# Normalising every tile in full before the turn, and finishing q at once, in a linear-attention and SwiGLU block

## Chip, cores, metric

One core of one Trainium2 chip (trn2). The metric is the device time of one execution in microseconds. The *span* of an execution is the stretch from its first to its last recorded instruction; the time is a little longer than the span.

## The reference, cut to what matters

```python
xn = layernorm(x)                                  # x: 2048 x 512, bf16
q, k, v = split(xn @ wqkv)                         # 32 heads of 16
phi = lambda t: where(t > 0, t + 1, exp(t)) + 1e-6
kv = einsum("bhsd,bhse->bhde", phi(k), v)
z  = sum over s of phi(k)
o  = (phi(q) kv) / (phi(q) z + 1e-6)
return x + o @ wo + (silu(xn @ w_gate) * (xn @ w_up)) @ w_down
```

The kernel works on 16 tiles of 128 rows. For the front of the program, each tile is normalised, turned (its columns must lie on the partitions), projected to k and q, and k and q go through phi. `G = xn^T phi(k)` is summed over the tiles in four PSUM banks. Then follow 56 gate and up groups, the division and the output tiles.

## The kernel before

The program is a list of operations; each engine runs its own in the order of the list and waits for what it depends on. The front is one text of letters with tile numbers. The letters that matter: S statistics, R 1/std, L/P/A normalise on VectorE/POOL/ACT, D turn by a DMA transpose, K/k and Q/q project to k and q, x/m/s phi of k (exp on ACT, min on POOL, sum on VectorE), y/n/u the same for q, z park q, G the G matmuls of a tile, F fillers.

```python
CENTRED = (0, 1)
NWARM = 8
...
def centre_half(t, h):                 # x - mean only: needs no 1/std
    K.add("dve", lambda e: e.tensor_scalar(
        out=xc[:, t, h * H:(h + 1) * H], in0=x_sb[:, t, h * H:(h + 1) * H], scalar1=mv[:, t, 0:1], scalar2=None,
        op0=ALU.subtract), r=xk(t) + [("mv", t)], w=[("xc", t, h)])
...
def nextbank():                        # projections share banks 4 to 7 in turn
    ring[0] += 1
    return 4 + (ring[0] - 1) % 4
...
def phi_keep(t):                       # park q in fp32, so that the bank comes free
    b, slot = at[0, t], later[t]
    K.add("act", lambda e: e.activation(tq[slot], banks[b][:, :], ACT.Copy), r=[B(b)], w=[("tq", slot)])

def phi_exp(i, t):
    ...
    if t in CENTRED:                   # the missing 1/std enters here
        K.add("act", lambda e: e.activation(buf, banks[b][:, :], ACT.Exp, bias=lstd[:, t:t + 1], scale=rstd[:, t:t + 1]),
              r=[B(b), ("rs", t), ("lstd", t)], w=[bkey])
    else:
        K.add("act", lambda e: e.activation(buf, banks[b][:, :], ACT.Exp), r=[B(b)], w=[bkey])
...
run("""
    S0 R0 b0 a0 d0 S1 M1 c0 F4 r0 C1 R1 g0 J0 W1 f0 K0 S2 r1 v1 k0 o1 S3 J1 R2 K1 x0 k1 L2 Q1 o0 x1 S4
    X2 m0 Q0 Y2 q1 m1 s0 R3 q0 R4 k2 L3 y1 s1 D3 P4 G0 S8 x2 z1 m2 D4 q2 S12 R8 z0 s2 G1 P8 y0 S14 G2
    ...
    s7 m6 q6 y7 L0 u8 D0 n7 q11 y6 s6 n6 G13 u7 y11 u6 n11 G5 u11 G14 u9 G11 u2 u1 G8 u0 G15 G7 G9 G10
    G4 G6
""")
```

Tiles 0 and 1 are only centred, and turned and projected so; the scale 1/std comes in afterwards, in phi and in a second, scaled copy for G. They are normalised again later, since the gate stage needs them. q of tiles 0, 1, 2, 8 and 9 is parked, and its sum runs late.

## Time and profile before

| | before |
|---|---|
| time, median of the first 3 executions | 213.36 us (213.19 to 213.69) |
| profiled execution | time 212.38 us, span 211.1 us |
| TensorE busy in the span | 98% |
| first projection | 6.09 us |
| first gate matmul | 48.09 us |

TensorE streams from the first projection on, one matmul of 512 columns each 0.216 us. So a hole in that stream, or a later start, is time lost, and work on the other engines is worth what it does to the stream. The lines that carry this are in the prediction.

### The profile page before, as it was taken

How to read it: one execution, taken by the hardware profiler on the slowest of the kernel's cores; microseconds unless marked ns; L12 is line 12 of the kernel's file. 1: busy time of each engine (PE TensorE's matmuls, PEld its weight loads, DVE VectorE, ACT ScalarE, POOL GpSimd, SP SyncE). 2: the span in 40 equal slices, each digit the busy share in tenths (PEclk: the TensorE clock that was granted, in tenths of full speed). 3: DMA queues.
4: the chain of work that ended last, by engine and by line, in shares of the span. 5: the costliest groups of instructions: out<-in, count | busy, mean ns of one | idle time of the engine just before them, and what ended most of it. 6: DMA issues, size and time to landing. Idle time of an engine off the chain costs nothing.

```text
span 211.1 us, 2717 instructions
## 1 busy us (share of the span) xinstructions
PE 207.3 (98%) x989; PEld 96.5 (46%) x1008; DVE 133.7 (63%) x225; ACT 69.8 (33%) x145; POOL 66.1 (31%) x91
## 2 busy tenths in 40 slices
PE   8999999999999999999999999999999999999996
PEld 3444444444544444444444444444444444444455
DVE  3998998965765379746546585755648754625122
ACT  4999986306363333031221322130123031220000
POOL 3789887999200252202202121202202220000000
PEclk9999999999999999999999999999999999999999
DMA  6954541499911301112011021011010111011101
GB/s 185 357 129 101 72 82 26 116 380 374 354 46 25 53 0 27 31 41 53 0 50 26 23 30 50 0 50 25 28 50 0 26 50 50 6 47 28 47 25 53
DMA packets 28829, 16.43 MB, mean 78 GB/s; under 512 B 18576, under 2 KB 28688, under 8 KB 28816
## 3 DMA queue, kind: packets, MB, share of 16 engines
q1 hardware_dynamic: 27984, 15.54, 27.3%
q10 hardware_dynamic: 832, 0.72, 1.0%
q8 instruction: 8, 0.13, 0.3%
q14 instruction: 5, 0.04, 0.1%
HBM read 9.96 MB, written 2.10 MB: 57 GB/s over the span
## 4 chain that ended last, share of the span: by engine, by line
PE 94%; DVE 2%; POOL 1%; issue 1%; ACT 1%; DVEq 0%
PE pb L521 45%; PE pb L619 23%; PE pb L390 10%; PE pb L615 6%; PE pb L439 6%; PE pb L247 2%; PE pb L357 1%; DVE stats L257 1%; POOL ef L418 1%; DVE pk L429 1%; ACT ef L411 1%; PE pb L546 1%; PE pb L609 0%; POOL xn L345 0%; DVE pq L429 0%
## 5 line engine op out<-in xcount | busy, mean ns | idle before, releaser
L529 ACT ACTIVATE sil<-pb 128x512 bf16<-128x512 f32 x56 | 33.3, 597 | 102.4 <-PE pb L521 98.7
L534 DVE TENSOR_TENSOR hT<-pb,sil 128x512 bf16<-128x512 f32 x56 | 38.2, 689 | 42.6 <-PE pb L521 39.9
L521 PE MATMUL pb<-xnT,wu 128*128 128x512 bf16 x223 | 57.5, 379 | 0.1
L521 PE MATMUL pb<-xnT,wg 128*128 128x512 bf16 x216 | 57.2, 379 | 0.4
L579 POOL TENSOR_TENSOR pz<-pq,zbc 128x512 f32<-128x512 bf16 x16 | 22.2, 1390 | 97.8 <-DVE den L586 79.6
L619 PE MATMUL pb<-wd,hT 128*128 128x512 bf16 (+2 forms) x249 | 51.0, 355 | 0.2
L619 PEld LDWEIGHTS pb<-wd,hT 128*128 128x128 bf16 x252 | 23.6, 98 | 24.9
L521 PEld LDWEIGHTS pb<-xnT,wu 128*128 128x128 bf16 x224 | 21.8, 98 | 26.4 <-DVE hT L534 1.4
L521 PEld LDWEIGHTS pb<-xnT,wg 128*128 128x128 bf16 x224 | 21.9, 98 | 25.8
L625 DVE TENSOR_TENSOR out_sb<-pb,x_sb 128x512 bf16<-128x512 f32 (+2 forms) x18 | 11.4, 632 | 23.1 <-PE pb L619 23.1
L390 PE MATMUL pb<-wqkv,xnT 128*128 128x512 bf16 x109 | 24.8, 379 | 0.2
L598 DVE TENSOR_TENSOR pq<-pq,rden 128x512 bf16<-128x512 bf16 x16 | 20.7, 1292 | 0.6
L418 POOL TENSOR_SCALAR ef<-ef 128x512 bf16<-128x512 bf16 x25 | 15.6, 628 | 4.3 <-ACT ef L411 3.9
L390 PEld LDWEIGHTS pb<-wqkv,xnT 128*128 128x128 bf16 x112 | 10.9, 98 | 13.3 <-DVE pk L429 0.5
L615 PE MATMUL pb<-M,pk 128*128 128x512 bf16 (+2 forms) x69 | 16.4, 354 | 0.2
L411 ACT ACTIVATE ef<-pb 128x512 bf16<-128x512 f32 x25 | 14.7, 591 | 3.5 <-PE pb L390 3.4
L257 DVE BATCH_NORM_STATS2 stats<-x_sb 128x6 f32<-128x512 bf16 x16 | 10.8, 677 | 3.3 <-DMA x_sb<-in_A_x_dram 3.1
L439 PE MATMUL pb<-pk,xn 128*128 128x512 bf16 x55 | 12.7, 379 | 0.1
L586 DVE TENSOR_REDUCE den<-pz 128x32 f32<-128x512 f32 x16 | 10.8, 675 | 0.0
L462 POOL TENSOR_TENSOR zacc<-zacc,pk 128x512 f32<-128x512 f32 x8 | 10.2, 1277 | 0.6
L615 PEld LDWEIGHTS pb<-M,pk 128*128 128x128 bf16 x72 | 6.8, 98 | 7.4
L429 DVE SCALAR_TENSOR_TENSOR pk<-pb,ef 128x512 bf16<-128x512 f32 x14 | 9.5, 681 | 1.0 <-POOL ef L418 0.8
(74 smaller groups left out, 111.3 us busy)
## 6 DMA issues: line engine op xcount, KB each, us to landing
out_dram<-out_sb SPq DMA_DIRECT2D x15, 128.0 KB, 1.9
x_sb<-in_A_x_dram SPq DMA_DIRECT2D x14, 128.0 KB, 4.3
wg<-in_B_w_gate_dram SPq DMA_DIRECT2D x2, 896.0 KB, 8.4
wu<-in_B_w_up_dram SPq DMA_DIRECT2D x2, 896.0 KB, 9.8
wd<-in_B_w_down_dram SPq DMA_DIRECT2D x2, 896.0 KB, 14.0
wqkv<-in_A_wqkv_dram ACTq DMA_DIRECT2D x2, 256.0 KB, 4.4
wqkv<-in_A_wqkv_dram SPq DMA_DIRECT2D x2, 256.0 KB, 4.7
wqkv<-in_A_wqkv_dram SPq DMA_DIRECT2D x1, 512.0 KB, 7.8
```

The source lines that it names most:

```text
L257: K.add("dve", lambda e: e.bn_stats(stats[:, t, :], x_sb[:, t, :]), r=xk(t), w=[("st", t)])
L390: K.add("pe", [(lambda e, c=c: e.matmul(banks[b][:, :], src[:, c, t * P:(t + 1) * P], wqkv[:, c, col:col + D], start=(c == 0), stop=(c == ...
L411: K.add("act", lambda e: e.activation(buf, banks[b][:, :], ACT.Exp), r=[B(b)], w=[bkey])
L418: K.add("pool", lambda e: e.tensor_scalar(out=buf, in0=buf, scalar1=top, scalar2=0.0, op0=ALU.min, op1=ALU.max), r=[bkey] + tkeys, w=[bkey])
L439: K.add("pe", [(lambda e, c=c: e.matmul(banks[c][:, :], src[:, t, c * P:(c + 1) * P], pk[:, t, :], start=first, stop=last)) for c in range ...
L521: fns.append(lambda e, c=c, b=b, w_=w_: e.matmul(banks[b][:, :], w_[:, c, fc * P:(fc + 1) * P], xnT[:, c, C * 512:(C + 1) * 512], start=(c ...
L529: K.add("act", lambda e: e.activation(sil[:, j % 2, :], banks[gb(j)][:, :], ACT.Silu), r=[B(gb(j))], w=[("sil", j % 2)])
L534: K.add("dve", lambda e: e.tensor_tensor(out=hT[:, C % 2, fc, :], in0=banks[gb(j) + 1][:, :], in1=sil[:, j % 2, :], op=ALU.mult), r=[B(gb( ...
L579: K.add("pool", lambda e: e.tensor_tensor(out=pz[:, t % 2, :].rearrange("q (g p) -> q g p", g=NG), in0=pq[:, t, :].rearrange("q (g p) -> q ...
L598: K.add("dve", lambda e: e.tensor_tensor(out=heads(pq[:, t, :]), in0=heads(pq[:, t, :]), in1=rden[:, i, :][:, :, None].broadcast_to([P, NH ...
L615: fns = [(lambda e, g=g: e.matmul(banks[bank][:, 0:hi - lo], pk[:, t, g * P:(g + 1) * P], M[:, g, lo:hi], start=(g == 0), stop=False)) for ...
L619: fns = [(lambda e, fc=fc: e.matmul(banks[bank][:, 0:hi - lo], hT[:, C % 2, fc, jj * P:(jj + 1) * P], wd[:, fc, lo:hi], start=False, stop= ...
```

## The change

The intent is a simpler front: every tile is normalised in full and then turned, and q of every tile is turned into phi at once. No centred tile, no parked copy, none of the small powers of std. The warm-up has ten matmuls instead of eight, the fillers are two instead of four, and the order of the whole front is a new one. Two DMA transposes fewer are issued, since tiles 0 and 1 are turned only once. The diff, cut to its core:

```diff
-CENTRED = (0, 1)
-NWARM = 8
+NWARM = 10
...
         def transp(t, b, lo=0, hi=NDC):
             tb = tview(b, hi - lo)
-            src = xc if t in CENTRED else xn
...
-        def phi_keep(t):
-            b, slot = at[0, t], later[t]
-            K.add("act", lambda e: e.activation(tq[slot], banks[b][:, :], ACT.Copy), r=[B(b)], w=[("tq", slot)])
...
         def phi_exp(i, t):
             b = at[i, t]
-            if t in CENTRED:
-                K.add("act", lambda e: e.activation(buf, banks[b][:, :], ACT.Exp, bias=lstd[:, t:t + 1], scale=rstd[:, t:t + 1]),
-                      r=[B(b), ("rs", t), ("lstd", t)], w=[bkey])
-            else:
-                K.add("act", lambda e: e.activation(buf, banks[b][:, :], ACT.Exp), r=[B(b)], w=[bkey])
+            K.add("act", lambda e: e.activation(ef[:, b - 4, :], banks[b][:, :], ACT.Exp), r=[B(b)], w=[("ef", b - 4)])
...
         run("""
-            S0 R0 b0 a0 d0 S1 M1 c0 F4 r0 C1 R1 g0 J0 W1 f0 K0 S2 r1 v1 k0 o1 S3 J1 R2 K1 x0 k1 L2 Q1 o0 x1 S4
...
+            S0 R0 S1 L0 R1 L1 S2 T0 E0 F2 T1 V1 R2 L2 k0 k1 x0 m0 S3 T2 S4 x1 m1 E2 R4 s0 q1 R3 L4 k2 x2 N3 A3
+            q2 s1 m2 y1 S5 R5 G0 D4 S6 s2 n1 G1 q0 y2 G2 D3 u1 R6 q4 N5 A5 S8 y0 k3 n2 N6 A6 u2 k4 y4 x3 n0 x4
+            n4 m3 u0 m4 S13 D5 q3 R8 u4 s3 P8 D6 S7 k5 y3 R13 D8 n3 G3 s4 x5 k6 R7 S9 R9 N7 q6 G4 m5 A7 u3 s5
...
+            x12 m12 k13 k15 n11 x15 m15 u11 G10 x13 m13 s12 G11 q15 q14 y15 n15 s13 s15 k14 x14 m14 y14 q12 s14
+            G12 y12 n12 n14 u15 G13 G14 u14 u12 G15
         """)
```

(T turns a tile on TensorE, E and V copy the turned tile out on ACT and VectorE.) With the parked sums gone, the G groups stand between the projections from the first tile on.

## The prediction

> **What bounds the kernel now.** I read first the page's shares, then the chain of work that ended last, then the order of time of the opening, then a table of stretches.
>
> ```profile
> PE 207.3 (98%) x989; PEld 96.5 (46%) x1008; DVE 133.7 (63%) x225; ACT 69.8 (33%) x145; POOL 66.1 (31%) x91
> PE   8999999999999999999999999999999999999996
> ```
>
> TensorE is busy 98% of the span, in every slice. Since a busy PE need not be at its peak, the chain decides:
>
> ```profile
> PE 94%; DVE 2%; POOL 1%; issue 1%; ACT 1%; DVEq 0%
> ...
> 6.30 2.45 PE pb L390 x10
> 8.75 0.22 PE pb L357 x4
> 8.97 2.16 PE pb L390 x10
> ...
> 44.64 3.62 PE pb L439 x16
> 48.25 3.67 PE pb L521 x17
> ```
>
> Ten projection matmuls take 2.16 us: one each 0.216 us, with no hole. The other engines appear in the chain only between 15.5 and 23 us, while TensorE is busy anyway. So after the opening the time is a count of matmuls. From the first projection (6.09 us) to the first gate matmul (48.09 us) lie 128 projection and 64 G matmuls (16 tiles x 12): 192 x 0.2158 = 41.43 us, plus one turned tile in the middle (0.22 us) and 0.35 us because the first few ran slow: 42.0 us, just what lies between. Everything before 6.09 us is warm-up and the way to the first turned tile:
>
> ```profile
> 3.12 0.69 DVE L257 BATCH_NORM_STATS2 stats<-x_sb 128x6 f32<-128x512 bf16 x1 [3.12 <-DMA x_sb<-in_A_x_dram]
> 3.85 0.18 DVE L260 BATCH_NORM_AGGREGATE mv<-stats 128x2 f32<-128x6 f32 x1
> 4.07 0.48 DVE L289 TENSOR_SCALAR hT<-x_sb,mv 128x256 bf16<-128x256 bf16 x2
> 4.07 0.29 ACT L264 ACTIVATE lnv<-mv,eps 128x1 f32<-128x1 f32 x1 [1.99 <-DVE mv L260]
> 4.39 0.20 ACT L266 ACTIVATE rstd<-lnv 128x1 f32<-128x1 f32 x1
> 4.41 0.61 PE L357 MATMUL pb<-ident,hT 128*128 128x128 bf16 x4
> 5.52 0.48 DVE L367 COPY hT<-pb 128x256 bf16<-128x256 bf16 x2
> 6.09 2.65 PE L390 MATMUL pb<-wqkv,hT 128*128 128x512 bf16 x10
> ```
>
> Tile 0 is only centred (4.07), so it need not wait for 1/std (ready at 4.59); it is turned and copied in halves, and the first projection starts at 6.09.
>
> **What the Trainium skill says.** (1) "TensorE: Matmul & The Clock Gate", Part 1, says that the array starts at half clock and is released after a sustained busy window of about 3.4 us, which runs freely, so that the moment varies. The trace agrees: the warm-up matmuls stand 0.427 us apart, the projections at 6.09 and 6.52 too, and from about 6.8 us on the distance is 0.216. (2) Part 4 of the same page says that transposes do not count as busy in the same way. No run here shows it yet; it matters because the new opening keeps two fillers where four stood. (3) "ScalarE: Activation LUTs", What ACT_TABLE_LOAD costs: a pointer operand adds about 93 ns to an ACTIVATE. The trace agrees: the exp of a centred tile, with pointer scale and bias, took 771 ns against 591 without. (4) "PSUM — Partial Sum Buffer", the section on bank collisions, asks for guarding by bank. The kernel does so, so the ring of four projection banks can make TensorE wait for the sum of phi on VectorE.
>
> **The change, part by part.**
>
> Off the path. Removed: five copies of q to fp32 on ACT (5 x 594 ns = 3.0 us); five late sums on VectorE (3.3 + 2.4 us), which become ordinary ones (5 x 686 ns), a relief of 2.3 us; the scaled start of the z sum on POOL (0.7 + 1.2 + 1.57 us, replaced by one 1.28 us add); the small powers, floors and caps; the separate xg (2 x 762 ns on POOL) and the second normalising of tiles 0 and 1; two of 15 DMA transposes. All this lies beside TensorE, which the chain shows as the limit: worth nothing by itself.
>
> Warm-up: ten matmuls of 512 instead of eight (+2 x 0.427 us) end at 0.84 + 10 x 0.427 = 5.11 us; fillers two instead of four. This too lies before the data arrive.
>
> On the path: the way to the first projection. VectorE now runs statistics of 0, statistics of 1, normalise 0, normalise 1. Statistics of 0 end at 4.03 as before. Those of 1 start at once if x of tile 1 has landed (it had by 4.46, where it was used without a wait; earlier nothing shows): 0.73 + 0.18 us, to 4.9. Normalise 0 then (1/std, at 4.59, is already there) runs about 0.4 us, the duration of the normalising rows, to 5.27. The four transposes run 5.30 to 5.73, with about 0.2 us until the last result shows. The copy is now one ACT instruction of 0.60 us instead of two VectorE copies: 5.97 to 6.57. First projection at 6.6 us, against 6.09. From there 192 x 0.2158 + 0.22 us for turning tile 2, and 0.1 us slow running if the clock is released at 6.8 as before: 48.35 against 48.09, so **+0.25 us**.
>
> Tile 1: 1/std at 5.5, normalised to 5.9, turned behind the fillers from 6.15 to about 6.8, copied by VectorE after the statistics of tile 2, about 0.4 us, to 7.3. The first k takes TensorE to 7.5, so no hole. Tile 2: turned after both k, at 8.4; its ACT copy stands behind the exp of tile 1 (8.6 to 9.2) and ends at 9.7, while q of tile 1 keeps TensorE only to 9.5: hole **+0.25 us**.
>
> The four-bank ring: I followed the new order by hand, with exp 0.6 us, min 0.61, sum 0.69, statistics 0.8 to 0.9 and normalise 0.41, 0.77 or 0.80 by engine. A bank needs 0.2 + 0.6 + 0.61 + 0.69 and some passing of signals, about 2.25 us, and is wanted again after three other projections, 2.6 us, or more where G matmuls lie between. Where statistics stand ahead of a sum the sum comes late: I find holes of about 0.3 us at k of tile 5 (its bank waits for q of tile 4) and at q of tile 9 (for q of tile 8), elsewhere within 0.1 us. The parked q of before freed banks without VectorE in just this part. Taken as **+0.45 us**. Total load does not threaten it: VectorE 16 x 0.81 + 32 x 0.65 + 6 x 0.41 = 36 us of about 46 available, ACT some 32, POOL some 25.
>
> Uncertain items, at their mean: tile 1 landing later than 4.0 us, up to 0.4 us, **+0.2**; the clock released later, **+0.3** (second rival). The last four G wait for the late tiles' sums: from the end of k of tile 14 to its G lie three groups of four, 2.6 us, against 2.25 us: no hole expected, **+0.25** for what my hand count misses. After the gate stage starts nothing changes; the z adds on POOL start at 48.4 and need 9 x 1.28 us, to 60, and are wanted only around 64.
>
> Sum: 0.25 + 0.25 + 0.45 + 0.2 + 0.3 + 0.25 = 1.7 us; scaled down slightly, since a late start hides some later holes, 1.5 us: 213.36 + 1.5 = 214.9.
>
> **The rivals.** (a) VectorE becomes the bound of the front, since no q can be put off until after the projections:
>
> ```profile
> 10.00:15.00 5.00, 4.95 (x24) 2.29 (x24) 4.80 (x13) 4.87 (x13) 3.65 (x8) 1.00 0.60 155
> 20.00:25.00 5.00, 4.95 (x24) 2.25 (x24) 4.92 (x11) 4.64 (x15) 4.26 (x9) 1.00 0.61 85
> 40.00:45.00 5.00, 4.95 (x24) 2.25 (x23) 4.96 (x6) 0.00 (x0) 4.84 (x5) 1.00 0.98 319
> ```
>
> The columns are the stretch, its length, then PE, PEld, DVE, ACT and POOL busy. VectorE and ACT are nearly full between 10 and 25 us already; the parked sums fill VectorE at 40 to 45. For the rival: 2.3 us of work that ran late must run earlier. Against it: the same change takes work away, and busy time counts the overlap of neighbours (a sum of 0.69 us was followed by the next after 0.60). It would show as repeated waits of projections for sums, 2 to 5 us in all: 216 to 218. (b) The half-clock lasts a window longer, to about 10.2 us, because waits and transposes interrupt the warm-up (0.2 us before tile 0, possibly more). For: fewer fillers, and the skill's remark. Against: two more warm-up matmuls. It costs half of the matmul time between 6.8 and 10.2, 1.7 us, of which the hole at tile 2 takes back some 0.25: about 216.3. (c) The simpler front is faster, because removing some 3 us of ACT and 2.3 us of VectorE work removes waits. Against: TensorE has no waits after 6.09 us to remove, and nothing in the change takes matmuls from it; it could win only by starting before 6.09. It would give 213.
>
> **Range and chances.** Lower end: only the start and one hole count, +0.4, 213.8. Upper end: the late clock with the holes, or many ring waits, 217.3. Slower by 2% means above 217.6 and needs (a) and (b) in part together: 0.12. Faster by 2% would need 4 us from a TensorE that does not wait: 0.01.
>
> **What would show it.** First projection at 6.5 to 7.0 us; spacing 0.216 from about 6.8 us; the first gate matmul at 49 to 50.5 us instead of 48.09, and from there to the end the same 163 us; in the waits, TensorE's weight loads of the projections waiting for the ACT copy of tile 2 and for VectorE sums, about 1 us in all. The prediction is wrong if the gate stage starts before 48.1, if spacing of 0.427 goes on past 8 us, if holes at the projections sum to over 2.5 us, or if the stretch after the gate start differs by more than 0.5 us.

## The result

| | before | after |
|---|---|---|
| median of 6 executions | 213.22 us (213.13 to 213.69) | 213.26 us (213.02 to 213.76) |
| ratio after/before | | 1.0003 (0.9987 to 1.0018) |
| profiled span | 211.1 us | 211.5 us |
| first projection | 6.09 us | 6.56 us |
| first gate matmul | 48.09 us | 48.50 us |

A ratio here and below is the mean time of one kernel's runs over that of the other's of the same rounds, with a 95% interval, so not quite the ratio of the medians quoted. The prediction, 214.9 us with a range from 213.8, was wrong.

The page of the kernel after, busy time and the slices of TensorE:

```profile
PE 207.6 (98%) x989; PEld 96.4 (46%) x1008; DVE 130.2 (62%) x219; ACT 69.2 (33%) x137; POOL 59.2 (28%) x80
PE   8999999999999999999999999999999999999996
```

3.5 us of VectorE and 7 us of POOL work are gone, TensorE is as full as before. The chain that ended last is 97% TensorE (94% before). The opening, in order of time (start, duration, engine, source line, operation, what it was idle for):

```profile
3.07 0.69 DVE L229 BATCH_NORM_STATS2 stats<-x_sb 128x6 f32<-128x512 bf16 x1 [3.07 <-DMA x_sb<-in_A_x_dram]
...
4.00 0.69 DVE L229 BATCH_NORM_STATS2 stats<-x_sb 128x6 f32<-128x512 bf16 x1
...
4.82 0.38 DVE L242 TENSOR_SCALAR xn<-x_sb,mv,rstd 128x512 bf16<-128x512 bf16 x1
...
5.26 0.61 PE L270 MATMUL pb<-ident,xn 128*128 128x128 bf16 x4
...
5.91 0.60 ACT L277 ACTIVATE xnT<-pb 128x512 bf16<-128x512 bf16 x1 [0.44 <-PE pb L270]
...
6.56 1.90 PE L298 MATMUL pb<-wqkv,xnT 128*128 128x512 bf16 x8
```

The steps of tile 0 fall within 0.1 us of the predicted times: normalise 4.82 (predicted 4.9), turn 5.26 (5.30), ACT copy 5.91 (5.97), first projection 6.56 (6.6). The second statistics did not wait for their tile. Eight projections took from 6.56 to 8.30: 0.2175 us each, so the half clock was over at 6.56, not at 6.8.

The stream after that:

```profile
8.52 3.02 PE L298 MATMUL pb<-wqkv,xnT 128*128 128x512 bf16 x12
11.37 1.89 PE L322 MATMUL pb<-pk,xn 128*128 128x512 bf16 x7
...
45.04 3.62 PE L322 MATMUL pb<-pk,xn 128*128 128x512 bf16 x16
48.50 1.03 PE L385 MATMUL pb<-xnT,wg 128*128 128x512 bf16 x4
```

Twelve projections stand between 8.52 and 11.37, 2.85 us where 12 x 0.2158 = 2.59 would do: one hole of 0.26 us. In the waits it is the weight load of k of tile 2, waiting for the ACT copy:

```profile
PEld pb L298 <- ACT xnT L277: 0.6, 1, 0.6
```

(0.6 us for the weight load, which runs ahead of its matmul.) From 11.37 to 48.50 lie 172 matmuls (192 less the 20 before): 172 x 0.2158 = 37.12 us, and 37.13 passed. **The four-bank ring made no hole at all.** The gate stage and all after it take the same 163.0 us as before. So in these two traces the change costs 0.41 us, in the opening (first projection 0.47 later, hole 0.26, less 0.32 because the first projections no longer run at half clock), and yet the times are equal.

That the two traces are not the whole story shows when spans and times of all executions are put side by side (all with a recorded span; the row of the kernel before has those that ran beside the experiments):

| kernel | executions | span: mean, lowest to highest | time minus span, mean | mean time |
|---|---|---|---|---|
| before | 50 | 211.92, 211.0 to 213.5 | 1.28 | 213.20 |
| after | 12 | 211.58, 211.3 to 212.0 | 1.80 | 213.38 |

Two things cross. The span of the kernel after is in the mean 0.34 us *shorter*: its best is 0.3 us worse than the best of the kernel before, but it lacks the long executions. And the part of the time outside the span is 0.52 us *longer*. The trace of the kernel before that I had read (211.1 us) is among the shortest: of the 50 spans only three are 211.1 or less, and their median is 211.8.

### The profile page after: what moved, and what is told of

It is laid out like the page before. It is cut to its first block, busy times and chain, and to the rows that moved or that the text cites. A ratio compares the mean times of both kernels' runs of the same rounds, so it can differ in the third digit from the quotient of the medians.

```text
span 211.5 us, 2678 instructions
## 1 busy us (share of the span) xinstructions
PE 207.6 (98%) x989; PEld 96.4 (46%) x1008; DVE 130.2 (62%) x219; ACT 69.2 (33%) x137; POOL 59.2 (28%) x80
## 4 chain that ended last, share of the span: by engine, by line
PE 97%; issue 1%; ACT 1%; DVE 0%; DVEq 0%
PE pb L385 45%; PE pb L478 23%; PE pb L298 13%; PE pb L322 7%; PE pb L474 6%; PE pb L219 2%; PE pb L410 0%; PE pb L270 0%; PE pb L468 0%; DVE hT L398 0%; ACT ef L306 0%; ACT xnT L277 0%; DVE out_sb L484 0%; DVEq L100 0%
## 5 line engine op out<-in xcount | busy, mean ns | idle before, releaser
L298 PE MATMUL pb<-wqkv,xnT 128*128 128x512 bf16 x126 | 29.2, 379 | 0.1
L310 POOL TENSOR_SCALAR ef<-ef 128x512 bf16<-128x512 bf16 x32 | 19.5, 614 | 19.3 <-ACT ef L306 19.1
L306 ACT ACTIVATE ef<-pb 128x512 bf16<-128x512 f32 x32 | 18.3, 591 | 9.6 <-PE pb L298 9.5
L298 PEld LDWEIGHTS pb<-wqkv,xnT 128*128 128x128 bf16 x128 | 12.3, 98 | 15.1 <-ACT xnT L277 0.6
L322 PE MATMUL pb<-pk,xn 128*128 128x512 bf16 x62 | 15.3, 379 | 0.2
L317 DVE SCALAR_TENSOR_TENSOR pk<-pb,ef 128x512 bf16<-128x512 f32 x16 | 10.8, 680 | 4.8 <-POOL ef L310 4.8
L317 DVE SCALAR_TENSOR_TENSOR pq<-pb,ef 128x512 bf16<-128x512 f32 x16 | 10.7, 682 | 3.9 <-POOL ef L310 3.9
```

The lines of the kernel that those rows point to most:

```text
L298: K.add("pe", [(lambda e, c=c: e.matmul(banks[b][:, :], xnT[:, c, t * P:(t + 1) * P], wqkv[:, c, col:col + D], start=(c == 0), stop=(c == ...
L306: K.add("act", lambda e: e.activation(ef[:, b - 4, :], banks[b][:, :], ACT.Exp), r=[B(b)], w=[("ef", b - 4)])
L310: K.add("pool", lambda e: e.tensor_scalar(out=buf, in0=buf, scalar1=1.0 + 1e-6, scalar2=0.0, op0=ALU.min, op1=ALU.max), r=[bkey], w=[bkey])
L317: K.add("dve", lambda e: e.scalar_tensor_tensor(out=dst, in0=banks[b][:, :], scalar=1e-6, in1=ef[:, b - 4, :], op0=ALU.max, op1=ALU.add), ...
L322: K.add("pe", [(lambda e, c=c: e.matmul(banks[c][:, :], xn[:, t, c * P:(c + 1) * P], pk[:, t, :], start=(t == 0), stop=(t == NT - 1))) for ...
```

## The experiments

Each kernel was correct. Those timed in one group share their runs of the kernel before.

### The two kernels again

No edit.

> The kernel before, once more. In its first trace the gate stage starts at 48.09 us, the span is 211.1 us, and that execution took 212.38 us, while the six timed ones took 213.13 to 213.69. Theory A (the profiled execution was an early one: what varies between executions is when the half clock ends): the spans here lie at 211.2 to 211.9, the typical one near 211.5, and this trace shows the first projections at a distance of 0.427 us for longer than to 6.8 us, or the gate stage at 48.3 to 48.5. Rival B (the trace was typical, and the kernel after owes its equal time to something after the gate start): spans near 211.1, gate start again at 48.1.

> The kernel after, once more. Theory A: spans 211.3 to 212.0 as in its first six, first projection at 6.5 to 6.6 us, gate stage at 48.5, time within 0.2 us of the kernel before. Rival B: time 0.3 us or more above the kernel before in these ten pairs, the first six being luck.

Measured: before_again 212.98 us median (212.47 to 214.45), spans 211.2, 212.7, 213.2, 212.0, 211.3, 211.3. after_again 213.37 us (213.04 to 213.71), ratio 1.0017 (0.9993 to 1.0041), spans 211.3 to 211.8. Theory A holds for the spans; the range of the kernel before is wider than I wrote. The profiled execution of before_again was again a short one (211.2 us, gate start 48.17), so this trace doesn't show a long execution.

### before_unparked: only the parking undone

```diff
-  ... S8 x2 z1 m2 D4 q2 S12 R8 z0 s2 G1 P8 y0 S14 G2
-  P1 D8 y2 S15 z2 q3 n2 R12 ...
+  ... S8 x2 n1 u1 m2 D4 q2 S12 R8 s2 G1 P8 y0 n0 u0 S14 G2
+  P1 D8 y2 S15 n2 u2 q3 R12 ...
```

(The same for tiles 8 and 9; the late n and u of these five tiles are dropped.)

> The kernel before with one part of the change: tiles 0 and 1 stay centred, but q of tiles 0, 1, 2, 8 and 9 is turned into phi at once instead of being copied to fp32 and finished late. My prediction (ring of four banks waits for VectorE) said 0.45 us for this part: gate start 0.3 to 0.6 us later and projections that wait for VectorE. Theory A (the ring has slack everywhere, parking only moved work): first projection at 6.1, gate start within 0.1 us of the kernel before, same time. Rival C (the order was tuned for parking, so each early sum pushes the others): gate start 1 to 2 us later.

Measured: 215.44 us, ratio 1.0120 (1.0092 to 1.0148), spans 213.9 to 215.2. Theory A falls, rival C holds: about 2.4 us in the mean of the spans. In order of time, two of the groups of projections that came late:

```profile
19.69 1.90 PE L390 MATMUL pb<-wqkv,xnT 128*128 128x512 bf16 x8 [1.10 <-DVE pq L429]
...
24.61 6.48 PE L390 MATMUL pb<-wqkv,xnT 128*128 128x512 bf16 x27 [0.42 <-DVE pq L429]
```

The bracket is the idle time of TensorE and what ended it: the sum of phi(q) on VectorE, which frees the bank. In the old order, with the sums at the places that I gave them, the parking was worth its five copies; other places were not tried. So the new kernel must have got rid of this wait in another way.

### after_glate: the G groups taken out from between the projections

```diff
-  ... k5 y3 R13 D8 n3 G3 s4 x5 k6 R7 S9 R9 N7 q6 G4 m5 A7 u3 s5
-  S12 x6 q5 G5 ... G6 ... q7 G7 ... G8 ... G9 ...
+  (the same without G3 to G9) ... q12 G3 G4 G5 G6 G7 G8 G9 s14
```

> The kernel after with the G matmuls of tiles 3 to 9 moved behind the last projection, as the kernel before has most of its G at the end; everything else in the order of the kernel after. Theory F (phi at once costs nothing there because G groups between the projections give the ring of four banks time): projections wait for VectorE sums, 1.5 to 3 us in all, gate start at 50 to 51.5 us. Rival G (the parking was never needed, the loss in before_unparked came from the places I put the sums at): gate start within 0.3 us of 48.5.

Measured: 218.22 us (five runs), ratio 1.0231 (1.0203 to 1.0259), gate start 53.55 us. Theory F holds, and more strongly than expected: from the first projection at 6.51 us to the gate start pass 47.04 us, against 41.65 us of work (192 x 0.2158 + 0.22), so 5.4 us of holes. Some of them, in order of time:

```profile
21.58 1.94 PE L298 MATMUL pb<-wqkv,xnT 128*128 128x512 bf16 x8 [0.35 <-DVE pq L317]
24.36 1.04 PE L298 MATMUL pb<-wqkv,xnT 128*128 128x512 bf16 x4 [0.85 <-DVE pk L317]
...
33.68 5.36 PE L298 MATMUL pb<-wqkv,xnT 128*128 128x512 bf16 x24 [1.48 <-DVE pq L317]
```

This is the same work by the same engines. With three projections between two uses of a bank the ring gives 2.6 us; a G group (0.86 us) in between gives 3.5. That is what the new order has in place of the parking. One thing this experiment does not separate: moving the G groups also packs the projections, and with them the work of VectorE, more closely. Between 20 and 35 us VectorE was busy 13.4 of 15 us here (12.8 in the kernel after), and 48 projection matmuls are recorded against 45. So the bank's turn-around and the pace of VectorE are both possible limits; that G groups in between remove the waits is shown, by which of the two is not.

### after_stats2: more work for VectorE in the new order

```diff
             bn1(t)
+            if t >= 5:
+                K.add("dve", lambda e: e.bn_stats(spare[:, t, :], x_sb[:, t, :]), r=xk(t), w=[("spare", t)])
```

> The kernel after with the VectorE statistics of tiles 5 to 15 computed twice (the second into a spare tile): 11 x about 0.65 us = 7 us more VectorE work in the front. In its trace VectorE waits about 9 us for the min of phi between 9 and 49 us, most of it after 29 us, while the statistics lie before 32. Theory L (little slack before 30 us, so a limit lies close): gate start 1.5 to 4 us later. Rival M (slack everywhere): under 0.5 us.

Measured: 216.72 us, ratio 1.0168 (1.0148 to 1.0188), gate start 52.23 in the trace, 3.7 us later than in the kernel after. Of that, 0.6 us is not from the edit: q of tile 1 waited for the q weights (second projections at 9.14 instead of 8.52). The rest, some 3.1 us, is in waits for sums, the longest at k of a tile around 28 us:

```profile
28.07 1.04 PE L299 MATMUL pb<-wqkv,xnT 128*128 128x512 bf16 x4 [0.91 <-DVE pk L318]
```

Theory L holds. VectorE is not the limit of the kernel after, but less than 7 us of work away from being it.

### before_normed: the centring undone, the parking kept

```diff
-CENTRED = (0, 1)
+CENTRED = ()
-  S0 R0 b0 a0 d0 S1 M1 c0 F4 r0 C1 R1 g0 J0 W1 f0 K0 S2 r1 v1 k0 o1 S3 J1 R2 K1 x0 k1 L2 Q1 o0 x1 S4
+  S0 R0 S1 L0 R1 L1 c0 e0 d0 f0 F2 W1 K0 k0 S2 v1 S3 R2 K1 x0 k1 L2 Q1 x1 S4
-  (later) P1 D1 ... L0 D0
```

(This also leaves two fillers instead of four, turns both tiles only once, and leaves TensorE idle for 0.88 us before tile 0.)

> The kernel before with the other part: tiles 0 and 1 are normalised in full before the turn (tile 0 turned and copied in halves, on ACT and VectorE), q still parked. By durations in the two traces the first projection starts at 6.15 to 6.3 us instead of 6.09, with a hole of up to 0.2 us before k of tile 1. Theory A (centring bought only the wait for 1/std): gate start 0.1 to 0.4 us later than in the kernel before of the same clock phase, time within 0.4 us. Rival D (centring is what kept TensorE full): 0.5 us or more.

Measured: 214.23 us, ratio 1.0039 (1.0003 to 1.0075), times 212.75, 212.85, 214.06, 214.4, 214.5, 214.76; spans 211.0, 211.1, then 212.3 to 212.9. So in two of six executions the span is as short as the best of the kernel before, and in four it is 1.2 to 1.9 us longer. The profiled one is of the long kind:

```profile
6.54 4.03 PE L390 MATMUL pb<-wqkv,xnT 128*128 128x512 bf16 x10
10.41 0.39 PE L357 MATMUL pb<-ident,xn 128*128 128x128 bf16 x4
```

Ten projections take from 6.54 to 10.41, 0.387 us each, where they should take 2.16 us: the half clock (0.427 us a matmul) lasted to about 10 us. This is what my second rival had forecast, in another kernel (whether the pause, the fewer fillers or the transposes bring it about is not separated here). The record's granted clock, 1.0 everywhere, does not show it; the distance of the matmuls does. Neither theory had foreseen it. Centring as such seems worth little: at its best the kernel without it loses nothing in span.

### after_longwarm: when does the half clock end?

```diff
-NWARM = 10
+NWARM = 24
```

> The kernel after with 24 warm-up matmuls instead of 10, to see the end of the half clock without gaps before it: the distance of the warm-up matmuls drops from 0.427 to 0.216 us at some moment r. The last warm-up matmul is over at r + (24 - (r - 0.84)/0.427) x 0.216, so a later r makes the span longer by 0.49 of the delay. Theory A2 (the moment wanders freely from execution to execution over some 3 us, TensorE being busy without a pause): spans spread by 1 us or more over the six executions. Rival E (with an unbroken warm-up r is fixed and only pauses make it late): r near 4 to 5 us and spans within 0.5 us. Both: some 3 us slower than the kernel after.

Measured: 216.03 us, ratio 1.0125 (1.0098 to 1.0153), spans 213.8, 213.8, 214.0, 214.5, 214.7, 214.9. The weight loads of the warm-up:

```profile
5.49 0.15 PEld L219 LDWEIGHTS pb<-const-bfloat16-1.0 128*128 128x128 bf16 x1 [0.28 <-issue]
5.90 2.29 PEld L219 LDWEIGHTS pb<-const-bfloat16-1.0 128*128 128x128 bf16 x11 [0.26 <-issue]
```

Single loads 0.427 us apart up to 5.49; from 5.9 us eleven in 2.29 us. So r was 5.9 us in this execution. The spans spread by 1.1 us, which by the 0.49 of the expectation is 2.2 us of r, if the clock alone spreads them: an estimated 4.5 to 6.7 us. A second trace without a pause, that of after_2dma below, has the change earlier: its warm-up matmuls stand 0.427 us apart up to 2.92 us and 0.22 from 3.65 us on. Theory A2 holds: with no pause before it, the end of the half clock still wanders.

### Warm-up count, both ways

```diff
before_warm6, before_warm10, before_warm10_2:  -NWARM = 8    +NWARM = 6  or  +NWARM = 10
after_warm8, after_warm8_2:                    -NWARM = 10   +NWARM = 8
```

> The kernel before with 10 warm-up matmuls instead of 8. Its spans so far spread from 211.0 to 213.5 us (17 executions), those of the kernel after, which has 10, from 211.3 to 212.0 (12). Theory J (with 8, the pause and the transposes from 4.3 us on let the half clock last a window longer in some executions, and 10 close that): every span from 211.2 to 212.2, since the two more end at 5.11 and put the transposes of tile 0 about 0.6 us later, which costs the fast executions up to 0.4 us; mean span 211.5 to 211.8. Rival K (the spread belongs to the centred opening or to the transfers, not to the warm-up): spread as before, up to 213.

> The kernel after with 8 warm-up matmuls instead of 10, the counterpart. TensorE then waits from 4.3 to about 5.2 us for tile 0. Theory J: some of the six executions run at half clock to about 10 us, spans up to 213, others as now at 211.3. Rival K: all spans 211.3 to 212.0.

> The kernel before with 6 warm-up matmuls, so a pause from 3.4 to 4.4 us: a dose below the 8 it has. Theory J (pause and transposes in the opening let the half clock last a window longer in some executions): more than the quarter of executions seen with 8 above 212.2 us, some near 213.5, and if the profiled one is among them its first ten projections stand 0.427 us apart until 9 to 10 us. Rival K (the spread is from elsewhere, the arrival of the q weights for instance): spread as with 8, and a long span goes with a wait for weights instead.

> after_warm8 again, for the count: its six spans were 211.4 to 213.1, two of them above 212.0, where the kernels of this order with 10 warm-up matmuls have none in 28. Theory J: again one to three of six above 212.0. Rival K: none, the first two were chance.

> before_warm10 again, for the count: its six spans were 211.2 to 212.2. Theory J: again all at 212.3 or below. Rival K: a quarter of them above 212.2, as with 8 (10 of 39).

Measured, by spans (the ratios to the kernel before are 1.0021, 1.0006 and 1.0016 for before_warm6, _warm10 and _warm10_2, all with intervals that hold 1; 1.0040, 1.0012 to 1.0068, and 1.0055, 1.0024 to 1.0086, for the two after_warm8):

| order of | warm-up | executions | mean span | above 212.2 us |
|---|---|---|---|---|
| before | 6 | 6 | 212.33 | 5 |
| before | 8 (as it is) | 50 | 211.92 | 11 |
| before | 10 | 12 | 212.01 | 1 (213.1) |
| after | 8 | 12 | 212.30 | 6 |
| after | 10 (as it is, and in after_2dma, after_1dma, after_best) | 26 | 211.47 | 0 |

(The "28" in one expectation was a miscount; it is 26, or 32 with after_fast, none above 212.0.) In the new order theory J holds: 6 of 12 against 0 of 26. (Six of the twelve ran on chip 6, where no execution of this order with ten was timed; on chip 5 alone it is 2 of 6 against 0 of 14. The kernel before does not tell the chips apart: its mean spans lie between 211.8 and 212.1 in each group.) In the old order theory J holds downwards (5 of 6 with six). That ten make fewer long executions than eight is not shown there: 1 of 12 against 11 of 50 can be chance, and the mean span with ten is no shorter than with eight. The trace of before_warm6, span 212.4, is of the long kind:

```profile
6.06 3.90 PE L390 MATMUL pb<-wqkv,hT 128*128 128x512 bf16 x10
9.80 0.39 PE L357 MATMUL pb<-ident,xn 128*128 128x128 bf16 x4
```

The first ten projections take 3.74 us instead of 2.16. The trace of after_warm8_2, span 213.2, shows a second source of spread: TensorE was at half clock until about 9.4 us, *and* x of tile 1 came late, so that the first projection stood at 7.25 us:

```profile
4.68 0.69 DVE L229 BATCH_NORM_STATS2 stats<-x_sb 128x6 f32<-128x512 bf16 x1 [0.82 <-DMA x_sb<-in_A_x_dram]
```

The two together make its gate start 1.7 us late: 0.7 from the tile, 1.0 from the clock. A third source is the q weights: in five of the eleven traces of the new order (after_1dma, after_best, after_fast, after_stats2, after_warm8) TensorE waited 0.26 to 0.46 us for them, in that of the kernel after not at all.

A fourth shows in the two traces of the old order with ten warm-up matmuls, spans 212.0 and 211.8, near the median of the kernel before. Their opening is no later than that of the short trace (first G matmul at 11.03 and 10.95 us against 10.97), so the clock is not what makes them long. They lose 0.7 to 0.8 us at one place. In before_warm10:

```profile
20.53 4.48 PE L390 MATMUL pb<-wqkv,xnT 128*128 128x512 bf16 x20
25.62 3.61 PE L390 MATMUL pb<-wqkv,xnT 128*128 128x512 bf16 x16 [0.61 <-DMA xnT<-xn]
```

The same projections in the short trace of the kernel before, without a hole:

```profile
20.46 7.93 PE L390 MATMUL pb<-wqkv,xnT 128*128 128x512 bf16 x35
```

The projection of q of tile 9 waits for its turned tile. The DMA transpose of that tile, issued at 20.2 to 20.3 us, landed 5.2 and 5.1 us after its issue in these two traces, 4.2 and 4.4 in those of before and before_again; most of the others take 2.4 to 2.6. (The view of before_warm10_2 puts its wait down to a sum of q that ended at the same moment; in the short trace this projection started before that sum was over, so it did not need it.) From the first G matmul to the gate start pass 37.90 and 37.83 us in these two traces, 37.12 to 37.24 in the four other traces of the old order with the parking, and 37.12 or 37.13 in all nine traces of the new order in which the G groups and the work of VectorE are as in the kernel after. So the new order has no such hole in any trace. (How often the kernel before has it is not known.)

Ten warm-up matmuls hold the turn of tile 0 in the old order from 4.4 to 5.1 us, but the traces show no later first projection for it (6.03 and 6.24 us against 6.09 and 6.16). In the new order tile 0 is ready at about 5.2 us, and ten fit without cost.

### after_2dma and after_1dma: the half microsecond outside the span

```diff
+        spare = sb("spare", [P, 2, NDC, P], bf)
+            "d": lambda t: K.add("sp", lambda e: e.dma_start_transpose(out=spare[:, t % 2, :, :], in_=xn[:, t, :]),
+                                 r=[("xn", t)], w=[("spare", t % 2)], dma=True),
-  ... D12 m11 n13 s11 q11 y11 k12 D14 u13
+  ... D12 m11 n13 s11 q11 y11 k12 d0 d1 D14 u13        (after_1dma: d0 only)
```

> The kernel after with two more DMA transposes into a spare tile that nobody reads, so 15 as before instead of 13. The measured time is 1.22 to 1.40 us above the span in the kernel before and in before_unparked (15 transposes), 1.72 to 1.91 in the kernel after and before_normed (13). Theory H (that half microsecond outside the span goes with the number of transfers): the difference falls to about 1.27 us and the time by 0.5 us at the same span. Rival (it goes with something else in the program): still about 1.8.

> The kernel after with one spare transpose, so 14 instead of 13 or 15. Theory H1 (time outside the span falls by a like amount for each transfer): time minus span about 1.5 us. Theory H2 (a step): 1.25 or 1.8 us, as one or the other.

Measured: after_2dma 212.80 us, spans 211.3 to 211.8, time minus span 1.24 in the mean; ratio to before 0.9973 (0.9939 to 1.0006). after_1dma 212.71 us, spans 211.4 to 211.8, time minus span 1.29; ratio 0.9990 (0.9964 to 1.0016). Theory H holds, in its form H2: a step between 13 and 14 of these transfers, not a share for each. A transpose that nobody reads makes this kernel 0.5 us faster, without touching the span. In every kernel the difference goes the same way: 1.2 to 1.4 us with 14 or 15, 1.7 to 1.9 with 13. What does it is not shown: the transfers are one thing that changes, each has a semaphore of its own and instructions of its own, and nothing in a record lies outside the span.

### after_fast and after_best: an attempt to beat both

```diff
after_fast and after_best:  - ... S3 T2 S4 x1 m1 E2    + ... S3 T2 S4 E2 x1 m1
after_fast:                 - ... L1 S2 T0 E0 F2 T1    + ... L1 c0 d0 e0 f0 S2 F2 T1   (tile 0 in halves, ACT and VectorE)
after_best:                 the two spare transposes of after_2dma
```

> Two small changes to the kernel after: tile 0 turned and copied in halves (ACT and VectorE), and the ACT copy of tile 2 ahead of the exp of tile 1. By the durations in the trace: first projection at 6.2 us instead of 6.56, the hole of 0.26 us before k of tile 2 gone; gate start at 47.9 to 48.1 where the clock is released as early as in the kernel after. So 0.4 to 0.6 us less than the kernel after, and 0.2 to 0.6 us less than the kernel before in the mean. Rival: the first projections at 6.2 run at half clock and the gain shrinks to 0.2 to 0.3 us.

> An attempt to beat both: the kernel after with the two spare transposes (the time lies 0.5 us nearer to the span, as after_2dma showed) and with the ACT copy of tile 2 ahead of the exp of tile 1. The hole of 0.26 us before k of tile 2 should close unless the q weights, which in after_fast came only at 8.8 us, make another: gate start 48.2 to 48.5, span 211.1 to 211.6, time 212.4 to 212.9, so 0.4 to 0.9 us less than the kernel before. Rival: the weights or the later exp of tile 1 take the hole back, and it times as after_2dma, about 212.8.

Measured: after_fast 213.37 us, ratio 0.9997 (0.9974 to 1.0021), spans 211.2 to 211.7: no gain on the kernel after. Its first projection stood at 6.13 us as expected, but then

```profile
8.81 2.93 PE L298 MATMUL pb<-wqkv,xnT 128*128 128x512 bf16 x12 [0.33 <-DMA wqkv<-in_A_wqkv_dram]
```

q of tile 1 waited for its weights. They are the next thing that the opening meets, and an earlier start can be handed to them; as the traces with late weights above show, their arrival also varies by itself. My expectation named them for after_best and not here, where they bit. after_best 212.50 us (212.36 to 212.86), ratio to the kernel before 0.9976 (0.9956 to 0.9997), spans 211.0 to 211.5, gate start 48.22: the best version, a quarter of a per cent, with the interval just clear of 1; it is the best of several that were tried. The kernel before has 15 transposes too, so against it the gain lies in the span: 211.18 us in the mean against 211.80 in the same rounds. Against the kernel after it is 0.86 us in the mean, 0.46 of it the step outside the span.

## Why the prediction was wrong, step by step

- **What bounds the kernel; work beside TensorE is worth nothing by itself.** Right. VectorE lost 3.5 us and POOL 7 us of work, and in these two traces the stream from the first G matmul on has no hole before or after.
- **Start of the first projection, 6.6 us; +0.25 us.** Right (6.56). The term measured +0.15: 0.47 later, less the 0.32 us of half clock that the projections of the old trace had.
- **Hole at k of tile 2, +0.25 us.** Right (0.26, by the ACT copy, as said).
- **Four-bank ring, "Taken as +0.45 us", and +0.25 us "for what my hand count misses".** Wrong: both terms measured 0.0 (37.13 us for 37.12 us of matmuls). At 0.70 us this is the largest wrong term. Waits for sums do exist elsewhere: 2.4 us in before_unparked, most of 5.4 us in after_glate. The following by hand used statistics of 0.8 to 0.9 us and sums of 0.69, where the trace has them start 0.80 and 0.60 us apart, and so may have piled up a lateness that was not there (not tested). The step I did not take was to ask what the new *order* does for the ring: the G groups between the projections give it 0.86 us each.
- **Tile 1 landing late, +0.2 us.** Not in the traces of the kernel after; seen once (0.82 us, after_warm8_2). A real spread; no trace of the old order shows it.
- **Clock released later, +0.3 us.** Wrong: no execution of the kernel after was of the long kind (12 spans, 211.3 to 212.0), and in both its traces full clock is reached by the first projection. I had listed the two more warm-up matmuls as "before the data arrive", that is, as worth nothing; in the new order they are worth 0.7 us of mean span (212.30 with eight, 211.58 with ten).
- **The base of the sum.** Wrong. I compared the new opening with one trace of the kernel before and put the difference on the median of *other* executions. That trace had a span of 211.1; the mean of 50 is 211.92. What makes the others longer is open, since no execution of that kernel with an ordinary span was profiled. Two things are shown in kernels of its order: the half clock lasting to between 9 and 10 us (before_normed, before_warm6), and a DMA transpose landing late (before_warm10 and before_warm10_2). The second needs no long half clock, and the 39 spans up to 212.2 still average 211.68, so the half clock alone need not be the answer.
- **What the sum left out.** A step of 0.52 us outside the span, which goes with two transfers fewer. The prediction saw the two transposes go and put them down as worth nothing. Nothing in the first profile could have shown it, save that time and span differ by 1.28 us.

Put together: of the 1.7 us summed, 1.2 us (ring 0.70, clock 0.3, tile 1 0.2) measured nothing in the traces of the kernel after, and 0.41 us remained; the gate stage, forecast at 49 to 50.5 us, began at 48.50. In means over executions, the opening's +0.4, the step outside the span of +0.52 and a gain of about 0.75 in the span make +0.2 us, inside the noise of either ratio. The 0.75 is not measured by itself: it is what is left when the mean span is 0.34 us shorter in spite of the 0.41. That the three cancel to "same" is luck. Of the rivals, (a) and (b) forecast things that were met, waits for sums and a long half clock, but only in experiments and not in the kernel after. Rival (c) named the right number, 213, for a reason that does not hold: the short trace of the kernel before had no waits for the change to remove, and the first projection did not start earlier.

Open: why the time outside the span has a step between 13 and 14 transposes; what share of the long executions of the kernel before is half clock, late transposes or late loads; and why one of twelve executions of the old order with ten warm-up matmuls was long all the same.

## What to carry to other kernels

Before a difference of a few tenths between two traces is put on a median, compare the span of the traced execution with the timed ones: a trace is one draw, and here it was an unusually good one. When a buffer is released late, look first at what else can stand between two uses of it in the order of the program; in the new order the G groups between the projections stand where the old one needed five parked tiles. And a warm-up is a trade between the time at which the data come and the odds that the clock is still at half rate then; it is read from the distance of matmuls, over many executions.

## What the Trainium skill lacked or had wrong

- "TensorE: Matmul & The Clock Gate", Part 1, puts the change of clock at about 4 us into sustained activity, give or take 500 ns, and elsewhere on the page calls it variable from run to run. Here, with TensorE busy without a pause from 0.84 us, it came at 3.65 us in one trace (after_2dma) and at 5.9 us in another (after_longwarm); after a shorter warm-up and a pause it came at 9.4 us (after_warm8_2) and at about 10 us (before_normed). The wander is wider than 500 ns. What the page lacks is how the odds go with the length of the warm-up: in the new order 6 of 12 long executions with eight matmuls, 0 of 26 with ten.
- No page tells of a part of the measured time outside the first and last instruction that steps with the number of transfers ("Runtime: NRT & Kernel Launch" has stages around a kernel, but no such step): 1.24 to 1.36 us in the mean with 14 or 15 DMA transposes in the front, 1.76 to 1.84 with 13.
